# Seven products instead of eight for half a batch, one wait of a block sum cut to what it reads, and a new order table

## The chip, the cores and the metric

The kernel runs on one core of a Trainium2 chip. The metric is the device time of one execution in microseconds (us), the median of several runs. A core has five engines that run side by side, each working through its own instructions in order: TensorE (PE in the profile; its weight loads are PEld), VectorE (DVE), ScalarE (ACT), GpSimd (POOL) and SyncE (SP). POOL and SP here do little but start transfers. The engines meet at semaphores.

## The reference, cut to what matters

Attention of 8 batches, 8 heads, 576 positions and head size 64, with a feature map in place of a softmax, then a feed-forward layer over all 4608 tokens.

```python
theta = pi / 2 * arange(S) / S
phi(x) = concat([relu(x) * cos(theta), relu(x) * sin(theta)])   # 64 -> 128
kv  = einsum('bhsf,bhsd->bhfd', phi(k), v);  z = sum(phi(k), over s)
num = einsum('bhsf,bhfd->bhsd', phi(q), kv); den = einsum('bhsf,bhf->bhs', phi(q), z) + 1e-6
x   = (num / den), heads side by side: 4608 tokens x 512
out = relu(x @ w_in) ** 2 @ w_out          # w_in 512 x 2048, w_out 2048 x 512
```

## The kernel before, in words

*Tiling.* Of each batch's 576 tokens 512 are "main" and 64 a "tail"; the tails of all 8 batches form a ninth batch (`b` = 8) of the feed-forward part. Main tokens are two sets of 256 (`tok` 0 and 1), made of the position groups `j` = 0 to 3. Inputs are float32; products run in bf16 and sum in PSUM.

*Attention of a batch b*, by the names of the steps: `ldk`, `ldq`, `ldv` load; `cos{b}.{j}` and `sin{b}.{j}` make the features, one instruction each on ScalarE or VectorE; `vs{b}.{i}` spreads v beside a column of ones; `kv{b}` is 40 matmuls, `kvz{b}` copies their sums out; `qT` turns the query features (on TensorE for batches 0 and 1, with a copy `qTc`; by a transposing DMA `qTd` on SP's queue later); `num{b}.{j}` is 8 matmuls; `div{b}.{j}` is three VectorE instructions; `xT` and `xTc`, later `xTd`, turn x. There is one PSUM buffer (pool `n`) for `kz` and `num`, so each `num` waits for the division before it.

*First matmul of the feed-forward part.* A plain block `H{b}.{s}.{tok}{half}` (`plan_plain1`) is 8 matmuls of 128x256 for 256 hidden units and 256 tokens, then a relu (`...r`) and for each two blocks a square (`...q`). A slice s takes four such blocks. Alternatively (`plan_gemm1`) a slice is done as a 2 x 2 block product in seven products `G{b}.{s}.P1` to `P7` of 4 matmuls each. These need sums of blocks of x (`xs{b}.1` to `4`, on VectorE) and of w_in (`w1s1` to `4`), and running sums that leave PSUM between products: `seed` and the copies `u2` and `s5`, then `c11` and `c21` (a relu) and `c12` and `c22` (a sum and a relu in one VectorE instruction). The tuple `PLAIN` names the (batch, half of the slices) that are done plainly; batch 0 always is.

*Second matmul.* `Y0.a0` to `a15` and `Y0.b0` to `b15` for batch 0: two matmuls of 128x512 each, for hidden block 0 to 15, for tokens set 0 (a) and 1 (b). Step n needs quarter n // 4 of w_out. Then `Y1` to `Y8` in seven products again, with sums `Y{b}.S1` to `S4` of activations and sums `w2t1` to `w2t4` of w_out (`plan_w2_sums`, L1333).

*PSUM* has a pool `x` of six banks for all else, `hps`, `ha`, `hb`, `hc`, transposes and second sums; a step that takes a bank waits for its last reader.

*What sets the order.* `ORDER` (L23 to L116) is a table of about 1070 step names. The planner `Plan.run` walks it: a word's star means ScalarE, and each engine gets its steps in the table's order. Its own durations and the given landing times of the first loads (for example q of batch 1 at 30.2, and the quarters of w_out at 27.4, 37.0, 41.9 and 45.2) only decide which buffer of a pool a step takes. The engines run their lists on the chip by semaphores.

*Start.* `begin()` does the first part of batch 0 by hand and puts on POOL's queue k tails, q and v of batch 0, four quarters of w_in (512 KB in bf16 each) and the first quarter of w_out. `loads_of_1()` puts there q and k of batch 1 with tails, w_out's second quarter, v of batch 1 and the last two quarters. It is called from the emission loop, not from the table:

```python
for o in order:
    ...
    o.emit(o.engine)
    if o in first:          # cos0.2, sin0.2, cos0.3, sin0.3
        first.remove(o)
        if not first:
            loads_of_1()
```

Loads of batch 2 are table words (`ldv2.0`, `ldk2`, ...) on POOL's queue too; from batch 3 on they stand on SP's. POOL's DMAs use eight semaphores in turn, so each waits for the one eight places before it to land.

Of the kernel before, what the change touches and what calls it, by code (L numbers as in the profile page):

```python
# [35 lines left out]
xT1.2 xTc1.2 Y0.a12 ldk2 Y0.a13 Y0.a14 Y0.b12 Y0.b13 w2t3 xT1.0 xTc1.0 Y0.a15 xTc1.1* vs2.0*
num1.3 Y0.b14 div1.3 Y0.c01* Y0.b15 Y0.c10* Y0.c11 Y0.c00* cos2.1 ldqt3 sin2.0 H1.3.00.0 sin2.1
cos2.3 xT1.3 xTc1.3* sin2.3 ldqt2 H1.3.00r* H1.2.00.0 H1.2.00r* ldkt2 H1.2.10.0 ldv2.1 vs2.1
H1.1.10.0 H1.1.11.0 H1.1.00.0 cos2.0* sin2.2* H1.0.11.0 H1.1.11r* H1.0.01.0 cos2.2* H1.1.00r*
ldkt3 sin2.tk* H1.2.10r* H1.3.10.0 H1.0.11r H1.3.10r* H1.2.01.0 Y0.st1 H1.1.10r* H1.0.01r  # L40
cos2.tk kv2 w2t2 w2t4 H1.1.11q H1.3.10q* kvz2* H1.2.01r* H1.0.10.0 H1.0.10r Y0.st0 qTd2.0
# [6 lines left out]
kv3 xTc1.4* H2.0.01.0 H2.1.00r xs2.4 Y1.c110* H2.0.00r* H2.1.00q* Y1.s5* G2.2.P1 H2.0.01r* kvz3
Y1.c22 G2.2.seed qTd3.0 num3.0 div3.0 cos3.tq* sin3.tq H2.1.11.0 H2.1.11r* H2.1.11q H2.0.10.0
H2.0.10r* num3.1 qTd3.1 H2.1.01.0 div3.1 Y1.P3 num3.2 H2.1.10q* ldq4 w1s3 G2.2.P2 Y1.c12  # L50
H2.1.01r* H2.1.01q* G2.2.P6 G2.2.c11r* div3.2 ldv4.0 G2.2.u2 G2.2.P5 G2.3.P1 ldk4 num3.3 div3.3
vs4.0* qTd3.2 ldkt4 G2.3.P5 G2.2.P7 G2.3.seed G2.2.s5* G2.2.c22r xTd3.0 G2.3.P2 G2.3.P6 G2.3.s5*
G2.3.P3 ldv4.1 G2.2.P4 G2.2.P3 G2.3.u2 G2.3.c11r* G2.3.P7 cos4.3 num3.4 G2.3.c11q Y2.P1 cos4.0
sin4.1* G2.2.c21r* G2.3.c22r G2.2.c12r sin4.0 cos4.1* cos4.2* G2.3.P4 G2.3.c21r xTd3.1 ldv5.2
G2.3.c12r sin4.2 xs3.1 sin4.3* ldkt5 Y1.st0 Y1.P4 Y2.seed G2.3.c21q* G2.3.c22q* G2.3.c12q Y2.S1
G3.0.P1 G3.0.seed qTd4.0 Y1.c21* qTd4.1 Y2.P2 G3.0.P2 xs3.2 G3.0.c11r* G3.0.P5 xs3.3 G3.1.P1
G3.0.P6 G3.0.s5* cos4.tk* G3.1.P5 Y2.S2 G3.0.u2* div3.4 G3.0.P3 Y2.P6 sin4.tk* vs4.1 kv4
G3.0.c12r Y2.u2 G3.1.seed G3.1.P2 Y2.S3 ldk5 G3.1.P6 vs5.2* kvz4* Y2.c11* Y2.S4 G3.0.P7 num4.0
G3.0.c22r ldv5.0 G3.1.c11r* G3.1.c11q* Y2.P5 xs3.4 G3.0.P4 G3.2.P1 div4.0 ldq5 G3.1.u2* G3.1.s5*
ldqt5 vs5.0* Y1.st1 G3.0.c21r num4.2 div4.2 G3.1.P3 Y2.s5 G3.1.P7 G3.1.c22r G3.1.c12r Y2.P7  # L60
num4.1 div4.1 ldqt6 G3.2.seed ldv5.1 G3.1.P4 G3.1.c21r* G3.2.P6 G3.2.u2* ldqt4 G3.2.P2 G3.2.c11r
sin5.0 Y2.c22 Y2.P3 Y2.c12 cos5.3* num4.3 G3.2.P5 G3.3.P1 G3.3.P5 cos5.1* xTd4.0 div4.3 xTd4.1
G3.2.s5* G3.3.seed G3.2.P7 G3.2.c22r G3.2.P3 G3.2.c12r sin5.1 G3.3.s5* G3.3.P6 Y2.st0 G3.3.u2*
cos5.0 qTd5.0 G3.3.P2 G3.3.c11r* G3.3.c11q G3.2.P4 G3.3.P3 G3.3.P7 Y2.P4 G3.3.c22r vs5.1* sin5.3
cos5.2 G3.1.c12q* G3.3.P4 Y3.P1 G3.1.c21q* G3.3.c21r G3.3.c12r G3.3.c12q sin5.2* kv5 xs4.1
G3.2.c21r* G3.3.c21q xs4.2 G4.0.P1 G4.0.P5 qTd5.1 ldv6.0 G3.3.c22q* Y3.seed Y3.P2 cos5.tq*
sin5.tq* kvz5* G3.1.c22q Y3.S1 Y3.S2 xs4.3 num5.0 div5.0 xs4.4 G4.0.seed G4.0.P2 G4.0.s5* ldv6.2
G4.0.P3 Y2.c21* G4.1.P1 G4.0.c11r* G4.0.P6 G4.0.u2* G4.0.c12r ldk6 Y3.S4 Y3.P6 ldq6 G4.1.seed
G4.1.P2 G4.1.c11r* G4.0.P7 G4.1.P6 G4.1.u2* G4.0.c22r vs6.2* num5.2 Y3.S3 G4.1.P5 G4.2.P1
Y3.c11* G4.0.P4 G4.1.P7 G4.1.s5* div5.2 Y3.P5 G4.1.c22r G4.1.c22q num5.3 div5.3 G4.1.P4 G4.1.P3  # L70
G4.0.c21r* G4.1.c12r Y3.u2* G4.2.seed G4.2.P6 G4.2.P2 vs6.0* G4.1.c21r* num5.1 G4.2.u2*
G4.2.c11r div5.1 G4.2.P5 G4.3.P1 G4.2.s5 ldkt6 sin6.3 sin6.0* qTd5.2 G4.3.seed Y2.st1 sin6.1
cos6.2* cos6.1* cos6.3* Y3.P7 Y3.s5 Y3.c22 G4.3.P6 G4.2.P3 cos6.0 G4.3.u2* xTd5.1 G4.2.P7
G4.2.c22r ldkt7 ldv6.1 G4.3.P2 xTd5.0 Y3.P3 G4.3.c11r* G4.3.c11q G4.3.P5 qTd6.0 G4.1.c21q*
G4.3.s5* G4.2.P4 G4.3.P7 Y3.c12 Y3.st0 G4.2.c21r* G4.3.P3 Y3.P4 sin6.2 qTd6.1 G4.3.c22r ldk7
G4.3.P4 G4.3.c12r vs6.1 G5.0.P1 xs5.3 ldv7.0 cos6.tk* sin6.tk* kv6 xs5.1 Y3.c21* G4.2.c12r xs5.2
G5.0.P5 G5.0.seed G5.1.P1 G5.0.P2 G4.1.c12q G4.3.c22q* ldq7 G4.1.c11q kvz6* G4.3.c21r num6.0
div6.0 G5.0.P6 G5.1.seed G5.1.P2 G5.1.P6 G4.3.c12q* Y4.S1 Y4.P1 G5.0.s5* Y4.S3 G5.0.u2* xTd3.2
num6.1 div6.1 G5.0.P3 G5.0.c12r G5.0.c11r* G4.3.c21q* Y4.S2 Y3.st1 G5.0.P7 Y4.seed Y4.P2
G5.1.c11r* ldqt7 xs5.4 G5.1.P5 G5.2.P1 G5.1.u2* G5.0.c22r G5.1.P7 num6.2 div6.2 G5.1.s5*  # L80
G5.1.c22r G5.1.P3 Y4.c11* G5.1.c12r vs7.0 G5.1.c22q* G5.0.P4 G5.0.c21r Y4.P6 Y4.u2* G5.2.P5
G5.2.s5* num6.3 G5.1.P4 ldv7.1 G5.2.seed G5.1.c11q Y4.P5 cos7.2* G5.2.P6 G5.1.c21r* G5.2.u2*
div6.3 Y4.S4 G5.2.P2 G5.2.c11r* cos7.3* cos7.1 G5.2.P3 sin7.2 G5.2.c12r Y4.s5* sin7.0 Y4.P7
# [1538 lines left out]
```

## Time and profile before

| | |
|---|---|
| median of 3 runs | 272.52 us (272.49 to 272.57) |
| the profiled execution | 271.95 us |
| its span, first to last instruction | 269.9 us |
| TensorE busy | 263.1 us (97%), 2787 matmuls |
| VectorE busy | 228.1 us (85%) |
| ScalarE busy | 186.7 us (69%) |
| POOL busy (it starts transfers) | 26.9 us (10%) |
| DMA | 51.23 MB, mean 190 GB/s |
| granted TensorE clock | 1.00 throughout |

Busy time counts from an instruction's start to its end, and matmuls overlap, so a busy TensorE says little by itself; whether it waits is seen from the starts of its matmuls. "Released by" says which engine or transfer ended a wait. The chain of waits is followed back from the last instruction, at each step to what let it go. In a timeline row the first two numbers are start and length in us, and the brackets give idle time before and what ended it. A DMA row of issues ends with the median time from issue to landing.

### The profile page before, as it was taken

Reading aid. Unit: us, or ns where it says so; the run is one execution under the profiler, and the core shown is the slowest. Engines: PE = TensorE matmul, PEld = TensorE weight load, DVE = VectorE, ACT = ScalarE, POOL = GpSimd, SP = SyncE. Lnnn points to the kernel's source line nnn. Section 1 sums busy time; section 2 is a strip of 40 time slices with the busy share of each in tenths; the row PEclk is TensorE's granted clock in tenths of the full one; section 3 lists DMA queues with packets and bytes.
Section 4 is the critical chain, followed back from the end, with each engine's and each line's share of the span. In section 5 each row is a group of like instructions: output and inputs, shape, how many; then the busy total and the mean of one; then the engine's idle time right before and its main releaser. Section 6 shows DMA issues by size and latency. Waiting matters only on the chain.

```text
span 269.9 us, 6751 instructions
## 1 busy us (share of the span) xinstructions
PE 263.1 (97%) x2787; PEld 225.0 (83%) x2792; DVE 228.1 (85%) x412; ACT 186.7 (69%) x289; POOL 26.9 (10%) x44
## 2 busy tenths in 40 slices
PE   8899999999999999999999999999999999999994
PEld 3568856699899889989998998899888888888883
DVE  3877987889998999999999999899978858797941
ACT  4762695698888997689699868587658636755510
POOL 8934443200000000000000000000000000000000
PEclk9999999999999999999999999999999999999999
DMA  6999999999899999999899998652540111010115
GB/s 221 220 206 253 328 198 250 298 295 298 221 247 314 221 261 298 300 183 231 284 275 209 232 359 208 152 155 100 61 125 15 38 63 78 8 72 2 78 50 186
DMA packets 82367, 51.23 MB, mean 190 GB/s; under 512 B 53217, under 2 KB 78817, under 8 KB 82337
## 3 DMA queue, kind: packets, MB, share of 16 engines
q1 hardware_dynamic: 71008, 38.28, 55.5%
q0 software_dynamic: 10736, 12.00, 21.2%
q10 hardware_dynamic: 592, 0.52, 0.6%
q8 instruction: 22, 0.36, 0.6%
q14 instruction: 9, 0.07, 0.1%
HBM read 36.70 MB, written 9.44 MB: 171 GB/s over the span
## 4 chain that ended last, share of the span: by engine, by line
PE 83%; DMA 12%; POOL 3%; issue 0%; DVE 0%; POOLq 0%
PE ya L461 18%; PE yb L461 16%; PE hb L461 13%; PE ha L461 8%; PE hc L461 8%; PE hps L461 8%; DMA w1sb<-in_moe_w_in_dram 5%; DMA kq<-in_k_dram 4%; PE num L461 3%; DMA w2sb<-in_moe_w_out_dram 3%; PE kz L461 3%; PE yc L461 3%; PE yh L461 3%; POOL kq L509 1%; POOL w1sb L411 1%; POOL v L1378 1%
## 5 line engine op out<-in xcount | busy, mean ns | idle before, releaser
L461 PEld LDWEIGHTS <-w1sb 128*128 128x128 bf16 x736 | 70.4, 98 | 8.6
L461 PEld LDWEIGHTS <-gs 128*128 128x128 bf16 x512 | 49.9, 98 | 5.8
L461 PEld LDWEIGHTS <-gT 128*128 128x128 bf16 x448 | 43.1, 98 | 9.8 <-issue 0.2
L442 ACT ACTIVATE gT<-gT 128x1024 bf16<-128x1024 bf16 x38 | 39.5, 1059 | 3.4 <-DVE gT L455 1.8
L461 PE MATMUL hps<-xT,w1sb 128*128 128x256 bf16 x320 | 37.4, 273 | 0.0
L448 ACT ACTIVATE fe<-kq,cols 128x1024 bf16<-128x1024 f32 (+1 forms) x39 | 35.1, 950 | 2.8 <-DMA kq<-in_k_dram 1.7
L461 PEld LDWEIGHTS <-w1s 128*128 128x128 bf16 x312 | 29.7, 98 | 3.3
L461 PE MATMUL ya<-w2sb,gT 128*128 128x256 bf16 x256 | 30.7, 273 | 0.0
L461 PE MATMUL hb<-xs,w1sb 128*128 128x256 bf16 x208 | 30.6, 273 | 0.0
L450 DVE TENSOR_SCALAR fe<-kq,cols 128x1024 bf16<-128x1024 f32 (+1 forms) x41 | 26.9, 690 | 4.0 <-DMA kq<-in_k_dram 4.0
L461 PE MATMUL ha<-xT,w1sb 128*128 128x256 bf16 x176 | 26.2, 273 | 0.0
L444 DVE TENSOR_TENSOR gT<-gT 128x1024 bf16<-128x1024 bf16 x34 | 23.2, 686 | 1.2 <-ACT gT L436 0.8
L436 ACT ACTIVATE gT<-ha 128x512 bf16<-128x512 f32 x21 | 12.6, 601 | 15.9 <-PE ha L461 15.9
L633 DVE TENSOR_TENSOR xp<-num,den 128x512 bf16<-128x512 f32 (+1 forms) x33 | 22.2, 675 | 1.1
L436 ACT ACTIVATE gT<-hps 128x512 bf16<-128x512 f32 x26 | 15.4, 602 | 8.1 <-PE hps L461 8.0
L455 DVE CUSTOM_DVE_ANT_0 gT<-hb,s 128x512 bf16<-128x512 f32 x26 | 17.8, 686 | 3.7 <-PE hb L461 3.3
L458 DVE TENSOR_TENSOR gs<-gT 128x2048 bf16<-128x2048 bf16 x16 | 19.4, 1219 | 0.4
L455 DVE CUSTOM_DVE_ANT_0 gT<-hc,u 128x512 bf16<-128x512 f32 x26 | 17.7, 683 | 0.8 <-PE hc L461 0.8
L432 ACT COPY hb<-ha 128x512 f32<-128x512 f32 x26 | 15.2, 585 | 4.3 <-DVE gT L438 1.8
L461 PE MATMUL hb<-xs,w1s 128*128 128x256 bf16 x104 | 15.6, 273 | 0.0
L436 ACT ACTIVATE gT<-hb 128x512 bf16<-128x512 f32 x18 | 10.8, 599 | 7.0 <-PE hb L461 4.5
L461 PE MATMUL hc<-xs,w1s 128*128 128x256 bf16 x104 | 15.6, 273 | 0.0
(120 smaller groups left out, 415.7 us busy)
## 6 DMA issues: line engine op xcount, KB each, us to landing
out_dram<-y SPq DMA_DIRECT2D x16, 512.0 KB, 3.7
vs<-in_v_dram SPq DMA_DIRECT2D x10, 512.0 KB, 4.8
kq<-in_k_dram SPq DMA_DIRECT2D x5, 1024.0 KB, 7.1
...
```

The costliest lines, as they stand in the source:

```text
L411: nc.gpsimd.dma_start(out=w1sb[:, :, f0:f1], in_=moe_w_in[:, f0:f1].rearrange("(kb p) f -> p kb f", p=P),)
L432: (nc.scalar.copy if e == "ACT" else nc.vector.tensor_copy)(out=out, in_=in_)
L436: nc.scalar.activation(out=out, in_=in_, func=ACTF.Relu)
L442: nc.scalar.activation(out=out, in_=in_, func=ACTF.Square)
L444: nc.vector.tensor_tensor(out=out, in0=in_, in1=in_, op=ALU.mult)
L448: nc.scalar.activation(out=out, in_=in_, func=ACTF.Relu, scale=col)
L450: nc.vector.tensor_scalar(out=out, in0=in_, scalar1=0.0, scalar2=col, op0=ALU.max, op1=ALU.mult)
L455: nc.vector._custom_dve(dve_ops.TENSOR_ADD_SAT, out=out, in0=in0, in1=in1, s0=BIG, s1=0.0)
L458: nc.vector.tensor_tensor(out=out, in0=in0, in1=in1, op=op)
L461: nc.tensor.matmul(out=out, lhsT=lhsT, rhs=rhs, start=start, stop=stop, skip_group_check=True)
L509: eng.dma_start(out=kq[b][:, "kq".index(nm)][:, hs, js], in_=main_of(nm, b)[:, hs, js])
L633: nc.vector.tensor_tensor(out=x, in0=n4[:, :, :, 0:D].rearrange("p b (k l) d -> p b k l d", l=2), in1=r.rearrange("p b (k l) -> p b k l", l=2)
```

## The change

1. `PLAIN` loses (2, 0): slices 0 and 1 of batch 2 are done by `plan_gemm1` instead of `plan_plain1`. The steps `H2.0.*` and `H2.1.*` go, and `G2.0.*` and `G2.1.*` come. The sum `w1s3`, which overwrites a block of w_in that plain blocks read, no longer waits for them but for those of batches 0 and 1 alone.
2. `w2t1`, the first block sum of w_out, waits for quarters 0 and 1 of w_out, which hold its two blocks; before it waited for all four.
3. The whole table `ORDER` is another one. Its beginning and the parts that the prediction speaks of:

```diff
-PLAIN = ((1, 0), (1, 1), (2, 0))
+PLAIN = ((1, 0), (1, 1))
...
-                w2_in + [made[a] for a in after] + (plain if n == 3 else []),
+                w2_in[: 2 if n == 1 else 4]
+                + [made[a] for a in after]
+                + (plain if n == 3 else []),
...
-sin0.2* xT0.k0 sin0.3 xT0.k2 cos0.2* qT0.2 cos0.3* qT0.3 xT0.k3 xTc0.k0 qTc0.2 num0.2 div0.2
-H0.1.00.0 xTc0.k2* H0.1.00.1 ldv2.0 H0.0.00.0 H0.0.00.1 xTc0.k3 xT0.2 qTc0.3* num0.3 H0.1.00.2
-H0.0.00.2 H0.2.00.0 div0.3 xT0.3 H0.3.00.0 xTc0.3 xTc0.2* H0.1.10.0 H0.1.10r H0.0.00r H0.1.00r*
+cos0.2* sin0.2* ldv2.0 xT0.k0 xTc0.k0* xT0.k2 sin0.3 xT0.k3 cos0.3 qT0.2 qT0.3 xTc0.k3*
+H0.0.00.0 qTc0.2 num0.2 xTc0.k2 H0.0.00.1 H0.0.00.2 H0.1.00.0 H0.1.00.1 H0.1.00.2 div0.2 xT0.2
+qTc0.3* xTc0.2* num0.3 H0.2.00.0 H0.2.00r* div0.3 xT0.3 xTc0.3 H0.3.00.0 H0.3.00r* H0.0.10.0
...
-Y0.a11 div1.1 num1.2 div1.2 Y0.b9 Y0.b10 Y0.b11 ldq2 w2t1 xT1.1 num1.0 H0.3.01q* div1.0 vs2.2
+sin1.1k cos1.tk* vs1.1 kv1 qTc1.2* H0.1.11q Y0.b8 Y0.b9 kvz1* num1.1 div1.1 Y0.a8 Y0.a9 ldv2.2
...
-num2.0 div2.0 vs3.0* Y1.P21 Y1.c111* Y1.S2 Y1.S3 cos3.1* ldv4.2 Y1.P5 cos3.0 sin3.0* sin3.1
-sin3.2 xTd2.1 num1.4 cos3.3* Y1.P6 H2.1.10.0 Y1.u2 H2.0.11.0 sin3.3* cos3.2 H2.1.10r* Y1.P7
+num2.0 Y1.S1 div2.0 Y1.P21 Y1.S2 ldq3 sin3.0* sin3.3* w1s3 Y1.P5 num1.4 div1.4 Y1.P6 Y1.u2*
+ldv3.1 vs3.1 xTd2.1 sin3.2 xT1.4 xTd2.0 xs2.1 sin3.1 xs2.2 Y1.c111 xs2.4 cos3.1* G2.0.P1 Y1.P7
+G2.0.seed G2.0.P6 xs2.3 G2.0.P5 ldqt3 cos3.0* G2.0.u2* G2.0.s5* xTc1.4* cos3.2 G2.0.P2
+G2.0.c11r* cos3.3 G2.0.P7 G2.0.c22r ldqt2 ldv4.2 G2.0.P3 G2.0.c12r G2.1.P1 G2.1.seed G2.0.P4
+G2.0.c21r* Y1.S4 G2.1.P5 G2.1.s5* G2.1.P2 G2.1.c11r* G2.1.P6 G2.1.u2* G2.1.P3 kv3 ldv4.0 kvz3*
+qTd3.0 G2.1.c11q G2.1.c12r cos3.tq* sin3.tq G2.1.P7 G2.1.c22r num3.0 div3.0 G2.2.P1 qTd3.1
```

More of the change, by code (lines that the diff above doesn't have):

```diff
@@ L36 @@
[L36 to L41, printed above, removed]
@@ L48 @@
[L48 to L53, printed above, removed]
@@ L54 @@
[L54 to L83, printed above, removed]
@@ new lines @@
+H0.1.00q H0.1.10r H0.1.10q H0.3.11.0 H0.3.11r f0.t1* w1s1 H0.3.10q* H0.1.01.0 H0.1.01r f0.t0*
+qT0.4 H0.1.11.0 H0.1.11r* H0.0.11.0 H0.0.11r* cos1.2q* H0.3.01.0 qTc0.4* sin1.1q sin1.2q*
+H0.3.01r Y0.a0 Y0.a1 Y0.a2 sin1.0q Y0.a3 cos1.3q cos1.0q* H0.2.11.0 qT1.0 qTc1.0 sin1.tq*
+H0.2.01.0 H0.2.11r cos1.tq* qT1.4 cos1.1q* qT1.1 qTc1.4 H0.2.01r* H0.3.01q cos1.3k* qT1.2
+cos1.2k* Y0.b0 Y0.b1 qTc1.1 sin1.tk* Y0.b2 sin1.2k* Y0.b3 H0.3.00q cos1.1k* H0.1.01q Y0.a4 Y0.a5
+Y0.b4 Y0.b5 Y0.a6 w1s2 sin1.0k Y0.a7 sin1.3k vs1.0* Y0.b6 vs1.2 Y0.b7 cos1.0k* sin1.3q* qT1.3
@@ new lines @@
+H1.1.11r* H1.0.10r* H1.1.10r* H1.1.01.0 H1.1.01r* H1.0.11r sin2.tk* H1.3.10.0 H1.1.11q Y0.st0
+H1.3.10r* H1.3.00q* H1.0.01.0 H1.0.01r* kv2 kvz2* H1.1.00.0 H1.2.10r* w2t4 H1.1.00r* H1.0.00.0
+H1.0.00r* H1.1.00q* H1.1.01q qTd2.0 num2.1 qTd2.1 H1.2.01.0 H1.1.10q H1.2.11.0 vs3.2* H1.2.01r*
+H1.3.10q div2.1 H1.2.11r* num2.2 H1.3.11.0 H1.3.11r* Y1.S3 ldv3.0 div2.2 vs3.0 H1.3.01.0
+H1.3.01r* H1.3.01q* Y1.P10 Y1.seed H1.3.11q num2.3 div2.3 Y1.P11 ldk3 Y1.seed1 Y1.P20 Y1.c110*
+num2.0 Y1.S1 div2.0 Y1.P21 Y1.S2 ldq3 sin3.0* sin3.3* w1s3 Y1.P5 num1.4 div1.4 Y1.P6 Y1.u2*
@@ new lines @@
+Y1.c12 num3.2 div3.2 G2.2.P2 G2.1.c21r* G2.1.c21q ldq4 G2.2.P6 G2.2.c11r* G2.3.P1 G2.3.P5 num3.3
+div3.3 G2.2.u2* G2.2.P7 G2.3.seed G2.3.P6 G2.3.P2 G2.2.c22r vs4.2 G2.3.s5* G2.3.P3 G2.3.u2*
+G2.3.P7 G2.2.P4 G2.3.c11r* G2.2.c21r* G2.2.P3 ldk4 cos4.1* G2.3.c11q ldkt4 sin4.1* Y2.P1
+G2.3.c22r G2.3.P4 qTd3.2 G2.3.c21r* Y2.seed xTd3.0 num3.4 cos4.0 G2.3.c21q* G2.3.c22q* sin4.0
+ldkt5 G2.3.c12r Y1.P4 xTd3.1 G2.2.c12r cos4.3 G2.3.c12q ldv4.1 sin4.3* G3.0.P1 G3.0.seed xs3.1
+G3.0.P5 Y1.c21* Y2.P2 cos4.2 ldqt4 G3.0.s5* G3.0.P2 G3.0.c11r* xs3.2 G3.0.P6 Y1.st0 G3.0.u2*
@@ L116 @@
+G8.3.P7 Y7.S3 G8.3.c11q* G8.3.c22r G8.1.c12q Y7.P3 Y7.c12 G8.3.c22q* G8.2.c21r* G8.3.P4 G8.3.P3
+G8.3.c12r G8.3.c12q* Y7.st0 Y8.P10 Y8.seed Y8.P11 G8.1.c22q Y8.seed1 G8.1.c21q* G8.3.c21r*
+G8.3.c21q* Y8.S1 Y8.S2 Y8.S4 Y7.P7 Y7.c22 Y8.P5 Y8.s5* Y8.P6 Y8.u2* Y8.P3 Y8.S3 Y8.P7 Y8.c22
+Y7.P4 Y7.c21* Y8.c12 Y8.st001 Y8.st011 Y8.st111 Y8.st101 Y7.st1 Y8.P4 Y8.c21* Y8.st110 Y8.st100
+Y8.P20 Y8.c110 Y8.st0010 Y8.st0000 Y8.P21 Y8.c111 Y8.st0100 Y8.st0110
 """
-PLAIN = ((1, 0), (1, 1), (2, 0))
+PLAIN = ((1, 0), (1, 1))
```

105 lines of the change are left out of this document (61 added, 44 removed).

## The prediction

> **What bounds the kernel now.** I read the page's busy shares first, then the waits of TensorE alone, then the chain of waits over the first 50 us, then the DMA queues in short stretches, and last the timeline of VectorE where the change puts its new work.
>
> ```profile
> span 269.9 us, 6751 instructions
> PE 263.1 (97%) x2787; PEld 225.0 (83%) x2792; DVE 228.1 (85%) x412; ACT 186.7 (69%) x289; POOL 26.9 (10%) x44
> ```
>
> ```profile
> PE wm L461 <- DVE zeros L362: 1.2, 1, 1.2
> PE tq L1428 <- DVE fe L450: 0.7, 1, 0.7
> PE num L461 <- ACT kvz L432: 0.2, 1, 0.2
> ```
>
> These three waits are all that TensorE shows, and all lie before 13 us. From 50 us on matmul follows matmul: I found no space between starts that is wider than the tile before it explains by more than 0.1 us. So every microsecond taken from TensorE's work is won and every new wait is lost, one for one. One place is an exception, in the chain of waits:
>
> ```profile
> 9.42 12.43 DMA w1sb<-in_moe_w_in_dram
> 21.85 0.28 issue
> 22.13 11.36 DMA kq<-in_k_dram
> 33.49 0.28 issue
> 33.77 9.04 DMA w2sb<-in_moe_w_out_dram
> 42.81 0.04 issue
> 42.85 0.38 PE yh L461
> ```
>
> The third quarter of w_out (operand `w2sb`) lands at 42.81 and TensorE starts its first product with it (`Y0.a8`) 0.04 later. Before it stood eight transposes from 42.14, 0.45 long, so TensorE was free at 42.59: 0.26 of waiting, too short for the list above. The queue that brings it is full. Queue q0, POOL's, in the stretches 14 to 18 us and 41 to 42 us (packets, MB, time as a share of 16 engines):
>
> ```profile
> q0 software_dynamic: 813, 0.81, 122.5%
> ```
>
> ```profile
> q0 software_dynamic: 199, 0.20, 120.7%
> ```
>
> Every stretch that I asked for between 14 and 43 us shows 105% or more for this queue. What is put into it early therefore delays all that stands behind.
>
> **The change, part by part.**
>
> *Fewer products.* Plain blocks of batch 2, slices 0 and 1 (`H2.0`, `H2.1`), were 8 steps of 8 matmuls; in seven products they are 14 steps of 4. That is 64 against 56. The chain prices 16 such matmuls (128x256) at 1.75, so 8 cost 0.87: the gain is 0.87 us on TensorE. Evictions grow: 8 (a relu each) become 14, the six new ones being copies (0.58 on ScalarE), and four relus become sums with a relu that only VectorE does (0.68). Squares stay 4. Over the kernel the built order gives ScalarE 13 instructions more and VectorE 7 fewer; VectorE's are cheap features and copies that moved to ScalarE. This costs nothing by itself where VectorE has room; where it has none, see below.
>
> *The first block sum of w_out.* `w2t1` now waits for two quarters instead of four. In the trace it started at 46.74 straight behind a division that ended at 46.83 and after the last quarter was there, and in the new table it stands later (behind `div1.3`). Nothing waited, so I price it at 0; a gain is excluded because VectorE runs in order, a loss because a wait only goes.
>
> *The table, start.* Up to the transpose `xT0.3` both orders give TensorE the same steps, but two quarter steps stood between `num0.3` and it and now stand ahead of it. By rows: division 1.13 plus 0.20 release, against 0.87 of cover (`H0.2.00.0`); `xT0.3` comes at about 20.8 instead of 20.61. This 0.2 is inside the 0.26 of idle time at 42.59, so 0.
>
> *The table, POOL's queue.* The loads of batch 1 are emitted when the four query features `cos0.2`, `sin0.2`, `cos0.3`, `sin0.3` are out. In the old table that is word seven, ahead of `ldv2.0`. In the new one `ldv2.0` (half of v of batch 2) is word three, and the built order shows it on POOL straight behind the first quarter of w_out, ahead of q1, k1, quarter two, v1 and quarters three and four of w_out. Its price: two equal loads that follow each other,
>
> ```profile
> 27.58 0.76 POOL L526 DMA_DIRECT2D vs<-in_v_dram x1 [0.83 <-DMA w2sb<-in_moe_w_out_dram]
> 30.56 0.74 POOL L526 DMA_DIRECT2D vs<-in_v_dram x1 [2.23 <-DMA kq<-in_q_dram]
> ```
>
> whose rows of issues say 9.9 and 8.2 to landing, so 37.5 and 38.8: 1.3 apart. The one before (a quarter of w_out, 25.97 and 10.2, so 36.2) leaves 1.35. I take 1.35. Low end 0, if the queue had holes, against which the shares above speak. High end 2.6: each POOL load also waits for the one eight places ahead, and with one more in the ring k1 waits for the fourth quarter of w_in (issued 10.15, 14.3 to landing) instead of the third (21.85); if its 11.36 were fixed and not time in the queue, everything would shift by those 2.6. First user of quarter three is now `Y0.b8`, with exactly as much TensorE work ahead of it as `Y0.a8` had. q1, too, is 1.35 later: `cos1.2q` at 31.65 on ScalarE, then `qTc0.4`, whose PSUM slot `H0.2.11.0` needs, and `cos1.0q`, which `qT1.0` needs: TensorE waits some 0.65 there, but that is earlier and so inside the 1.35. VectorE and POOL behind gain slack. Cost: 1.35.
>
> The Trainium skill, "DMA: Bandwidth & Descriptors", section "Anatomy of one DMA", puts a load of this path at 2.0 us fixed plus its bytes by 436 GB/s, an estimate of 3.2 for the 512 KB that are read here. Taken as time in the queue it would give 275.9 in place of my figure; the landings 1.3 apart say that the fixed part overlaps. The same page, section "SWDGE vs HWDGE vs iDMA", says only one such queue is allocated; the trace agrees, as its loads landed in order of issue.
>
> *The table, 70 to 88 us.* VectorE is full here already:
>
> ```profile
> 70.00:80.00 10.00, 10.00 (x112) 8.83 (x111) 9.86 (x16) 8.76 (x12) 0.00 (x0) 1.00 0.90 202
> ```
>
> (The stretch, its length, then busy time of PE, PEld, DVE, ACT and POOL, the clock, the DMA share and GB/s.) Starts follow each other like this:
>
> ```profile
> 71.05 0.16 DVE L627 TENSOR_SCALAR den<-num 128x8 f32<-128x8 f32 x1
> ...
> 72.09 1.22 DVE L458 TENSOR_TENSOR gs<-gs,gT 128x2048 bf16<-128x2048 bf16 x1
> 73.22 1.22 DVE L458 TENSOR_TENSOR gs<-gT 128x2048 bf16<-128x2048 bf16 x1
> 74.36 2.07 DVE L450 TENSOR_SCALAR fe<-kq,cols 128x1024 bf16<-128x1024 f32 x3
> ```
>
> A division is 1.04, a block sum 1.13, a feature 0.66, an eviction of 512 0.60, an x sum 0.33. Four waits of TensorE follow, each counted from the one before:
>
> (a) `G2.0.P6` needs the second x sum. VectorE from the end of `num2.3`: release 0.20, `div2.3` 1.04, `Y1.S1` 1.13, `div2.0` 1.04, `Y1.S2` 1.13, `w1s3` 1.13 (moved here from 87.18), `div1.4` 1.04, `vs3.1` 0.60, `sin3.2` 0.66, `xs2.1` 0.33, `sin3.1` 0.66, `xs2.2` 0.42, 0.05 to TensorE: 9.43. TensorE meanwhile: 3 x 0.87, 3 x 1.75, the two `num` 0.25 and 0.53, a transpose 0.22, `G2.0.P1` 0.44: 9.30. Late by 0.13.
> (b) `G2.0.P4` needs `G2.0.c22r`, behind `Y1.c111` 0.36, two x sums, two features and itself 0.68: 2.98 against 2.67. Late by 0.31.
> (c) `G2.1.P5` takes the bank that `G2.0.c12r` frees: 0.60 against 0.44. Late by 0.16.
> (d) `num3.0` needs `kvz3`: release 0.20, copy 0.59, 0.05, with one product (0.44) between. Late by 0.40.
>
> Sum 1.00. Low end 0.40: only (d) needs no queue of VectorE. High end 2.2: `G2.0.P1` now needs the transposes by DMA of both halves of x2 at about 77; the last is issued at about 73.9, and such rows run from 2.75 to 4.9 to landing, 1.2 late at worst. I take 1.00, since the 4.9 stood behind a v load that now goes earlier. `H2` steps that hid these chains (0.87 each with one eviction) are gone, so this cover is not there.
>
> *Later than 100 us.* Handovers with little cover (a product that waits for an eviction one product earlier) are as many and as short in the new order as in the old, which shows no wait. I price this at 0, with 0 to 0.5.
>
> Sum: -0.87 + 1.35 + 1.00 = +1.48. Against the profiled execution's own 271.95 (span 269.9 and 2.05 around it) that is 273.4; it stood 0.57 under the median of the runs, 272.52, so I predict 274.0.
>
> **The rivals.**
>
> *The shift is larger.* The ring of eight lets the delay grow to 2.6, or the transposes come 1.2 late: 275.2 to 275.3, both 276.5. For it: the chain runs over just those waits. Against: the queue holds several loads at each of them.
>
> *The early load is hidden.* Then -0.87 + 1.00 leaves +0.13: 272.65, no change. Against: shares over 105%.
>
> *The saving arrives: faster.* Place: VectorE's queue at `num2.3`. If features on ScalarE leave it with 0.6 us of slack there, (a) to (c) vanish, and with w_out on time only (d) stays: -0.47, 272.05; -0.87, 271.65, if `kvz3` is covered as well. It decides where lateness at `Y0.b8` and waits at 77 to 88 us sum to under 0.33. Against: 9.86 of 10 us busy.
>
> *The change does not do what it says*: true of `w2t1`, and worth nothing either way.
>
> **How the numbers follow.** Both delays as sized, within 273.3 to 274.9: 0.62. Larger shift: 0.19. Hidden load, about 272.4 to 273.0: 0.12. Faster: 0.07. Changes under 0.2% (0.54 us) are no change that a measurement of this kernel can tell. Hidden load splits, 0.07 to within and 0.05 to slower; so faster 0.07, same 0.07, slower 0.86. The range 272.6 to 275.7 leaves out the faster case, a part of the hidden load and the two mishaps together.
>
> **What would show it.** Right: `Y0.b8` starts at about 44.2, straight upon a landing of w_out; q1's first feature at 31.6; spaces between matmuls at 80 to 88 us that sum to about 1, with `num` waiting for `kvz`. Wrong: w_out's third quarter landing at 43 or earlier, TensorE without spaces at 77 to 88 us, or new ones beyond 100 us, which I did not price.

## The result and the profile after

The changed kernel takes 275.26 us (median of 4 runs, 274.75 to 275.78) against 272.50 for the kernel before in the same comparison: a ratio of 1.0099, 95% interval 1.0076 to 1.0123, or 2.76 us slower. The profiled execution took 275.01, 3.06 more than that of before. The page of the changed kernel:

```profile
span 272.9 us, 6743 instructions
PE 263.5 (97%) x2779; PEld 224.0 (82%) x2784; DVE 223.8 (82%) x405; ACT 191.1 (70%) x302; POOL 26.9 (10%) x44
```

The eight matmuls are gone (2787 to 2779), and yet TensorE is busy 0.4 longer: busy time hides both the saving and the waits. These are shown by the view of TensorE's waits, which before ended at 13 us (it counts only what exceeds a usual handover, so it reads lower than the spaces between starts that the text quotes):

```profile
PE kz L462 <- DVE vext L433: 0.6, 2, 0.4
PE num L462 <- ACT kvz L433: 0.5, 2, 0.2
PE tq L1431 <- ACT fe L449: 0.5, 1, 0.5
PE ha L462 <- DMA xT<-xp: 0.4, 1, 0.4
PE tx L657 <- DVE xp L634: 0.3, 1, 0.3
PE tq L652 <- ACT fe L449: 0.2, 1, 0.2
```

The rows `kz` and `tq L1431` and one of the two `num` lie before 13 us, where the two kernels do the same work. `tx` is the transpose `xT0.3` at 21.39, with a space of 0.51 ahead of it; `tq L652` is `qT1.0` at 34.68, 0.37; `ha` is `G2.0.P1` at 77.68, 0.55; the other `num` is `num3.0` at 87.07, 0.41. The chain of waits, which before ran over the third quarter of w_out, now runs over q of batch 1, then over a transpose of x2 by DMA, then over `kvz3`:

```profile
18.03 14.14 DMA kq<-in_q_dram
32.17 0.02 issue
32.19 0.54 ACT fe L449
...
73.27 4.37 DMA xT<-xp
77.64 0.04 issue
77.68 0.60 PE ha L462 x4
...
86.42 0.60 ACT kvz L433
87.03 0.04 issue
87.07 0.40 PE num L462 x8
```

The timeline of POOL's issues in the changed kernel (start, length, what is issued, and in brackets the time before it and what ended that) shows the early load between the first quarter of w_out and q1:

```profile
12.71 0.76 POOL L419 DMA_DIRECT2D w2sb<-in_moe_w_out_dram  x1 [0.30 <-DMA v<-in_v_dram]
15.16 0.75 POOL L527 DMA_DIRECT2D vs<-in_v_dram  x1 [1.70 <-DMA w1sb<-in_moe_w_in_dram]
18.03 0.90 POOL L510 DMA_DIRECT2D kq<-in_q_dram  x1 [2.12 <-DVE xT L433]
```

Last, a place that the prediction did not look at, the end. The timelines of VectorE and of SP's stores in the changed kernel (ScalarE's queue starts about as many stores, at nearly the same times):

```profile
262.79 0.69 DVE L459 TENSOR_TENSOR y<-yb,ys 128x512 f32<-128x512 f32 x1 [2.56 <-issue]
263.39 0.68 DVE L459 TENSOR_TENSOR y<-yc,yu 128x512 f32<-128x512 f32 x1
267.97 0.42 DVE L433 COPY y<-ya 128x256 f32<-128x256 f32 x1 [0.45 <-PE ya L462]
```

```profile
264.10 1.34 SPq L1107 DMA_DIRECT2D out_dram<-y  x2
265.53 0.62 SPq L1098 DMA_DIRECT2D out_dram<-y  x1
266.83 2.67 SPq L1107 DMA_DIRECT2D out_dram<-y  x3
```

and the same two in the kernel before:

```profile
259.16 0.69 DVE L458 TENSOR_TENSOR y<-yc,yu 128x512 f32<-128x512 f32 x1 [1.27 <-issue]
260.85 0.69 DVE L458 TENSOR_TENSOR y<-yb,ys 128x512 f32<-128x512 f32 x1 [1.00 <-PE yb L461]
266.09 0.42 DVE L432 COPY y<-ya 128x256 f32<-128x256 f32 x1 [0.45 <-PE ya L461]
```

```profile
259.88 2.31 SPq L1106 DMA_DIRECT2D out_dram<-y  x2
263.20 0.34 SPq L1097 DMA_DIRECT2D out_dram<-y  x1
264.95 2.07 SPq L1106 DMA_DIRECT2D out_dram<-y  x3
```

The new table puts `Y8.c12` (`y<-yc,yu`) behind `Y8.c22` (`y<-yb,ys`), `Y7.P4` and `Y7.c21`. Early stores that went out from 259.88 on now go out from 264.10 on and meet the last ones: the last three issues on SP take 2.67 in place of 2.07, the last store is issued 0.56 after its copy has ended (268.39 to 268.95; before 0.03, from 266.51 to 266.54) and lands 2.81 after its issue in place of 2.02. From the start of the last matmul to the end of the span it is 5.21 us, before 4.13.

So the 3.0 us of the span are: TensorE's last matmul 1.88 later, the end 1.08 longer. The 1.88 divide at the first product with w_out's third quarter, ahead of which both orders give TensorE the same work. It is now `Y0.b8`; the row of TensorE's timeline that starts with it:

```profile
43.98 1.02 PE L462 MATMUL yh<-w2sb,gT 128*128 128x512 bf16 x3
```

`Y0.a8` started at 42.85, so this is 1.13 later. From there to the last matmul 0.76 are lost, the saved 0.87 against 1.63 of new spaces, 1.49 of them between 70 and 90 us.

### The profile page after: what moved, and what is told of

Its sections match the earlier page's. It is cut to its first block, busy times and chain, and to the rows that moved or that the text cites. A ratio compares the mean times of both kernels' runs of the same rounds, so it can differ in the third digit from the quotient of the medians.

```text
span 272.9 us, 6743 instructions
## 1 busy us (share of the span) xinstructions
PE 263.5 (97%) x2779; PEld 224.0 (82%) x2784; DVE 223.8 (82%) x405; ACT 191.1 (70%) x302; POOL 26.9 (10%) x44
## 4 chain that ended last, share of the span: by engine, by line
PE 83%; DMA 10%; ACT 2%; POOL 2%; DVE 1%; issue 0%; POOLq 0%
PE ya L462 17%; PE yb L462 15%; PE hb L462 13%; PE hc L462 9%; PE ha L462 9%; DMA kq<-in_q_dram 8%; PE hps L462 5%; PE yh L462 4%; PE kz L462 3%; PE num L462 3%; PE yc L462 2%; DMA xT<-xp 2%; ACT fe L449 1%; PE tq L652 1%; POOL v L1381 1%; POOL kqt L513 1%
## 5 line engine op out<-in xcount | busy, mean ns | idle before, releaser
L462 PEld LDWEIGHTS <-w1sb 128*128 128x128 bf16 x704 | 67.2, 98 | 9.0 <-issue 0.9
L449 ACT ACTIVATE fe<-kq,cols 128x1024 bf16<-128x1024 f32 (+1 forms) x42 | 38.6, 959 | 2.9 <-DMA kq<-in_q_dram 1.6
L462 PEld LDWEIGHTS <-w1s 128*128 128x128 bf16 x336 | 32.3, 98 | 3.9 <-issue 0.2
L443 ACT ACTIVATE gT<-gT 128x1024 bf16<-128x1024 bf16 x31 | 32.3, 1059 | 1.6 <-DVE gT L456 1.1
L462 PE MATMUL hps<-xT,w1sb 128*128 128x256 bf16 x256 | 29.8, 273 | 0.2
L462 PE MATMUL ha<-xT,w1sb 128*128 128x256 bf16 x192 | 28.6, 272 | 0.4 <-DMA xT<-xp 0.4
L445 DVE TENSOR_TENSOR gT<-gT 128x1024 bf16<-128x1024 bf16 x41 | 27.6, 684 | 1.5 <-ACT gT L437 0.9
L451 DVE TENSOR_SCALAR fe<-kq,cols 128x1024 bf16<-128x1024 f32 (+1 forms) x38 | 23.6, 657 | 3.9 <-DMA kq<-in_k_dram 3.2
L433 ACT COPY u<-hb 128x512 f32<-128x512 f32 x21 | 12.4, 590 | 11.4 <-PE hb L462 11.4
L437 ACT ACTIVATE gT<-ha 128x512 bf16<-128x512 f32 x24 | 14.5, 605 | 5.2 <-PE ha L462 5.0
L433 ACT COPY s<-hc 128x512 f32<-128x512 f32 x24 | 14.1, 588 | 4.3 <-PE hc L462 4.3
L437 ACT ACTIVATE gT<-hps 128x512 bf16<-128x512 f32 x23 | 13.0, 598 | 5.9 <-PE hps L462 5.5
```

Of the source, the lines that this page charges most:

```text
L433: (nc.scalar.copy if e == "ACT" else nc.vector.tensor_copy)(out=out, in_=in_)
L437: nc.scalar.activation(out=out, in_=in_, func=ACTF.Relu)
L443: nc.scalar.activation(out=out, in_=in_, func=ACTF.Square)
L445: nc.vector.tensor_tensor(out=out, in0=in_, in1=in_, op=ALU.mult)
L449: nc.scalar.activation(out=out, in_=in_, func=ACTF.Relu, scale=col)
L451: nc.vector.tensor_scalar(out=out, in0=in_, scalar1=0.0, scalar2=col, op0=ALU.max, op1=ALU.mult)
```

## The experiments

Ratios are to the kernel before on the same chip, with a 95% interval. Waits and landings are those of one profiled execution each; executions of one kernel differ among themselves by 1 to 3 us, and when transfers land differs with them. Where a version is compared with the changed kernel, both intervals count, so such a difference is uncertain by some 0.9 us.

**The early load in the kernel before, alone.**

```diff
-sin0.2* xT0.k0 sin0.3 ...
+sin0.2* xT0.k0 ldv2.0 sin0.3 ...
...
-H0.1.00.0 xTc0.k2* H0.1.00.1 ldv2.0 H0.0.00.0
+H0.1.00.0 xTc0.k2* H0.1.00.1 H0.0.00.0
```

> The kernel before with one word moved: ldv2.0 becomes the table's third word, so POOL issues it ahead of the loads of batch 1. Theory: w_out's third quarter lands 1.3 us later, and as TensorE was at most 0.3 us short of it, the kernel is 1.0 to 1.4 us slower, 273.5 to 273.9. Rival (hidden load): within 0.3 us of 272.5.

Measured: 273.74, ratio 1.0054 (1.0036 to 1.0072), about 1.5 slower. The price is there, with nothing else of the change. The chain of waits of this run now goes over q of batch 1:

```profile
17.67 14.38 DMA kq<-in_q_dram
32.05 0.03 issue
32.08 0.72 ACT fe L449
32.80 0.49 ACT gT L437
33.29 0.04 issue
33.33 1.91 PE hps L462 x16
```

ScalarE runs in order: the relu (`gT`, L437) that frees TensorE's bank stands behind the first feature of q1, which waits for q1. TensorE waits 0.87 ahead of `H0.3.01.0`, and only some 0.15 at w_out's third quarter. Still it is this quarter that sets the price: issued at 35.47, it landed after 8.60, at 44.07 (before: 42.81), and `Y0.a8` started at 44.11, 0.04 later, just as before. By an estimate from these numbers, without the wait for q1 TensorE would have come there at about 43.1 and waited 1.0 instead of 0.15. The two waits stand in series, and the second is too short here for the chain to show it.

Landings counted from that of w_out's first quarter, which is ahead of them all, show the shift free of when an execution got going. In the seven profiled executions with the early load q1 landed 4.28 to 4.77 after it, in the seven without 2.91 to 3.47; the third quarter 15.9 to 17.3 after it against 14.5 to 15.5. In the mean each is 1.4 later. The Trainium skill's estimate quoted in the prediction (3.2 from "DMA: Bandwidth & Descriptors", "Anatomy of one DMA") is too large as the delay that a load brings to those behind it in this queue: that was 1.4 in the mean.

**The load put back in the changed kernel.**

```diff
-cos0.2* sin0.2* ldv2.0 xT0.k0 xTc0.k0* xT0.k2 sin0.3 xT0.k3 cos0.3 qT0.2
+cos0.2* sin0.2* xT0.k0 xTc0.k0* xT0.k2 sin0.3 xT0.k3 cos0.3 ldv2.0 qT0.2
```

> The changed kernel with one word moved: the first v load of batch 2 (ldv2.0) stands behind cos0.3 again, so POOL issues it behind the loads of batch 1 and w_out, as before the change. Theory of the prediction (w_out's third quarter held TensorE back by 1.35): 1.3 us faster than the changed kernel, about 273.9. Rival read from the trace of the changed kernel (the third quarter landed at 43.9 and TensorE came there at 44.2, so only the two waits on q1 at 33 to 35 us, 0.4 to 0.6 together, hang on the load): 0.4 to 0.6 faster, about 274.7. If the load were hidden: no change, 275.3.

Measured: 274.92, ratio 1.0092 (1.0070 to 1.0114): some 0.2 faster than the changed kernel, not 1.3 (the intervals admit 0.7 slower to 1.1 faster, so the rival's 0.4 to 0.6 stays possible). The rival rests on a start of `Y0.b8` at 44.2, but its first matmul is at 43.98, 0.13 after the landing, so by the trace the waits on q1 alone were worth some 0.1. From the view of TensorE's waits in it:

```profile
PE ha L463 <- DMA xT<-xp: 0.8, 1, 0.8
...
PE yh L463 <- DMA w2sb<-in_moe_w_out_dram: 0.3, 1, 0.3
```

In this execution there are 0.44 at `Y0.b8`, now waiting for the quarter of w_out as the kernel before did, and at `G2.0.P1` the space grew from 0.55 to 0.92. It was the longest of the six (276.01), so it doesn't show by itself where the gain of the others went; that it is lost at `G2.0.P1`, behind the early load in series, is borne out by the version with start, load and end put right.

**The end put back in the changed kernel.**

```diff
-Y8.P7 Y8.c22 Y7.P4 Y7.c21* Y8.c12 Y8.st001 Y8.st011 Y8.st111 Y8.st101 Y7.st1
+Y8.P7 Y8.c12 Y8.st001 Y8.st011 Y8.c22 Y7.P4 Y7.c21* Y8.st111 Y8.st101 Y7.st1
```

> The changed kernel with Y8.c12 and its two stores moved ahead of Y8.c22, as in the kernel before. Theory: the four early stores go out at about 261 and 264 us instead of 264.1 to 265.3, the last stores find a free queue, and the time from the last matmul's start to the end falls from 5.2 to about 4.1: 1.1 us faster, about 274.2. Rival: the long end is a chance of that one profiled execution, and the time stays within 0.3 us of 275.3.

Measured: 274.23, ratio 1.0067 (1.0047 to 1.0087), 0.9 faster than the changed kernel. From the last matmul to the end of the span it is 4.12, as in the kernel before. All other waits of the changed kernel are still there (0.51 at `xT0.3`, 0.78 at `G2.0.P1`, 0.41 at `num3.0`), and a new one came: 0.52 at 101 us, where `G3.0.P5` waits for an x sum of batch 3.

**The new end in the kernel before**, first with only half of it, then whole.

```diff
-Y8.P7 Y8.c12 Y8.st011 Y8.c22 Y8.st001 Y8.st111 Y8.st101 Y7.P4 Y7.c21* Y7.st1
+Y8.P7 Y8.c22 Y8.st111 Y8.st101 Y7.P4 Y7.c21* Y8.c12 Y8.st001 Y8.st011 Y7.st1
```

> The kernel before, with only the end of the table in the changed kernel's order: Y8.c12 and its stores behind Y8.c22, Y7.P4 and Y7.c21. Theory (the late copy crowds the last stores): the four early stores go out some 4 us later and meet the last ones on SP, the last store is issued late and lands later; last matmul to end of span grows from 4.1 to about 5.1 us, 1.0 slower than the kernel before. Rival (the 1.08 at the end of the changed kernel is chance of one profile, or comes from its later arrival there): no change, within 0.3 us.

Measured: 272.66 against 272.04, ratio 1.0017 (0.9999 to 1.0035); last matmul to end 4.37. The edit left the two stores `Y8.st111` and `Y8.st101` early. With these moved as well:

```diff
-Y8.P7 Y8.c12 Y8.st011 Y8.c22 Y8.st001 Y8.st111 Y8.st101 Y7.P4 Y7.c21* Y7.st1
+Y8.P7 Y8.c22 Y7.P4 Y7.c21* Y8.c12 Y8.st001 Y8.st011 Y8.st111 Y8.st101 Y7.st1
```

> The kernel before, with Y8.c12 and now all four early stores behind Y8.c22, Y7.P4 and Y7.c21, the very order of the changed kernel's end. Theory (four early stores, not two, have to go out late to crowd the last ones): they are issued from 2.8 us before the last matmul on, the last store lands late, last matmul to end of span some 5.2 in place of 4.1: 1.0 slower than the kernel before. Rival (the order of the copies is worth what moving two stores gave, 0.24 in the span and 0.5 in the time, and the rest of the changed kernel's 1.08 has another cause): 4.4 and 0.5 slower at most.

Measured: 272.96, ratio 1.0023 (1.0006 to 1.0040), 0.6 slower than before; last matmul to end 4.97. The mechanism holds: the more stores are left to the last 3 us, the later the last one lands. The interval admits 0.2 to 1.1, and 0.84 of the profile's 1.08 is reproduced.

**Start, load and end put right together in the changed kernel**, and one feature (`cos3.3`) that stood ahead of a sum TensorE needs.

```diff
-cos0.2* sin0.2* ldv2.0 xT0.k0 ...
+cos0.2* sin0.2* xT0.k0 ... cos0.3 ldv2.0 ...
-H0.0.00.0 qTc0.2 num0.2 ... H0.0.00.2 ... H0.1.00.2 div0.2 ... num0.3 H0.2.00.0
+qTc0.2 num0.2 H0.0.00.0 ... div0.2 ... num0.3 H0.0.00.2 H0.1.00.2 H0.2.00.0
-G2.0.c11r* cos3.3 G2.0.P7 G2.0.c22r ... G2.0.c12r
+G2.0.c11r* G2.0.P7 G2.0.c22r ... G2.0.c12r cos3.3
...
```

> The changed kernel with four moves in the table: ldv2.0 back, the tail's sums and stores ahead, at the start H0.0.00.0 behind num0.2 and H0.0.00.2, H0.1.00.2 behind num0.3 (as in the kernel before), and cos3.3 behind G2.0.c12r. Theory: 1.1 from the tail, 0.5 to 1.3 from the load, 0.3 from the start, 0.2 from the feature: 2.1 to 2.9 faster than the changed kernel, 272.4 to 273.2, near the kernel before; what is left against a gain of 0.87 are the waits for the transposes of x2 (0.55) and for kvz3 (0.4). Rival (the moves only shift waits): 274 or more.

Measured: 274.31, ratio 1.0067 (1.0046 to 1.0088): no better than the end alone. The wait 0.51 at `xT0.3` fell to 0.08, TensorE came to `G2.0.P1` at 76.3 instead of 77.1, and waited there for 1.34; 0.52 are again at `G3.0.P5`. Its chain of waits:

```profile
72.39 5.17 DMA xT<-xp
77.56 0.04 issue
77.60 0.60 PE ha L463 x4
```

This and the load put back say the same: what comes from ahead of 77 us is lost at `G2.0.P1`. Its start lay between 77.3 and 78.2 in all executions that have it in this place. The twelve times of this version lie between 272.7 and 275.1; the profile is of one at 274.37, and what was different in the fastest isn't known.

**Cover for that wait by order alone.** `G2.0.P1` behind `Y1.P7`, 1.75 of other work.

```diff
-cos3.1* G2.0.P1 Y1.P7
+cos3.1* Y1.P7 G2.0.P1
```

> The changed kernel, with only G2.0.P1 behind Y1.P7 instead of ahead of it, so that 1.75 us of other work cover the transposes of x2 by DMA. Theory (that wait costs one for one): the 0.55 at G2.0.P1 goes, G2.0.P6 behind it would come at 79.3 where its x sum is ready at 79.2, so nothing takes its place: 0.5 faster than the changed kernel, some 274.7. Rival (VectorE is full, so the wait moves on to G2.0.P6 and G2.0.P4, which need its x sums and its sum with a relu): no change, waits at these two that sum to 0.5 more.

Measured: 277.04, ratio 1.0165 (1.0136 to 1.0193), slower. The wait for x2 went, and two took its place, in the view of TensorE's waits from 70 to 90 us:

```profile
PE hb L463 <- ACT hb L434: 0.7, 1, 0.7
PE yb L463 <- ACT yu L434: 0.5, 1, 0.5
```

`Y1.P7` needs the copy `Y1.u2` of the step just ahead (a space of 0.67), and `G2.0.P6` needs `G2.0.seed`, the copy of what `G2.0.P1` has just made (0.82). With 0.23 at the next copy (`G2.0.u2`) and 0.48 at `G3.0.P5` that is close to the 1.8 by which it is slower than the changed kernel. In the table's order each of the two products covered the other's copy. Neither theory had this: the wait moved, but to ScalarE's copies, not to VectorE's sums.

**One product more between `kv3` and `num3.0`.**

```diff
-G2.1.P6 G2.1.u2* G2.1.P3 kv3 ldv4.0 kvz3* qTd3.0
+G2.1.P6 kv3 kvz3* G2.1.u2* G2.1.P3 ldv4.0 qTd3.0
```

> The changed kernel, with only kv3 and kvz3 one product earlier (ahead of G2.1.P3, 0.44 us), so that two products stand between kv3 and num3.0. The planner's buffers then differ for 101 later steps. Theory: the 0.41 at num3.0 goes and the division behind it starts 0.4 earlier too: 0.4 faster than the changed kernel, some 274.9. Rival (the chain of num and div of batch 3 is bound at its other end): the wait turns up at num3.1 or behind, no change.

Measured: 276.53, ratio 1.0148 (1.0122 to 1.0174), slower. The edit put `kvz3` ahead of `G2.1.u2` on ScalarE, and `G2.1.P7`, which needs `u2`, waited 0.89; `num3.1` waited 0.60 for VectorE. With `kvz3` left behind it:

```diff
-G2.1.P6 G2.1.u2* G2.1.P3 kv3 ldv4.0 kvz3* qTd3.0
+G2.1.P6 G2.1.u2* kv3 G2.1.P3 ldv4.0 kvz3* qTd3.0
```

> The changed kernel with kv3 alone one product earlier; its copy kvz3 stays behind G2.1.u2 on ScalarE, unlike in the run before. Theory A (num3.0 waits for the copy and for nothing else): the 0.41 goes and is won, 0.4 faster than the changed kernel. Theory B (VectorE is the bound there: G2.1.c12r, sin3.tq and G2.1.c22r stand ahead of div3.0 and one product later than before): div3.0 starts where it did, num3.1 waits some 0.45 in place of 0.08, no change from the changed kernel within 0.3.

Measured: 276.12, ratio 1.0133 (1.0107 to 1.0158), no gain. `num3.0` no longer waits, `num3.1` and `G2.1.P4` do (0.61 and 0.49). TensorE's waits from 80 to 95 us:

```profile
PE num L463 <- DVE xp L635: 0.4, 1, 0.4
PE hb L463 <- DVE gT L457: 0.3, 1, 0.3
```

Both are for VectorE, whose timeline has no gap from 86.14 on (and one of 0.81 just before, ended by a product of TensorE that now stands behind `kv3`):

```profile
86.14 0.69 DVE L457 CUSTOM_DVE_ANT_0 gT<-hc,u 128x512 bf16<-128x512 f32 x1 [0.81 <-PE hc L463]
86.75 0.48 DVE L452 TENSOR_SCALAR fet<-kqt,cols 128x512 bf16<-128x512 f32 x1
87.14 0.68 DVE L457 CUSTOM_DVE_ANT_0 gT<-hb,s 128x512 bf16<-128x512 f32 x1
87.74 0.16 DVE L629 TENSOR_SCALAR den<-num 128x8 f32<-128x8 f32 x1
```

`num3.0` ended at 86.56, and its division (last row) began 1.18 later, behind two sums and a feature; in the changed kernel it began 0.17 after the end of `num3.0` (87.34 to 87.51). Of the two, theory B names the mechanism: covering the copy alone doesn't win the 0.41, since VectorE comes to the division just as late. Its forecast of no change is not met as well; the median is some 0.9 slower than the changed kernel (interval 0 to 1.9), and the profiled execution (275.05) was the fastest of the five. And as VectorE was idle ahead of this stretch, it is the order of its steps that is late there; a division ahead of the two sums was not tried.

**All of the above together**, with two edits at 94 to 101 us (`ldkt5` behind `xTd3.1`, `Y2.P2` ahead of `G3.0.P5`).

> The changed kernel with all of it together: ldv2.0 behind cos0.3, the old order of the last copies, two quarter steps of batch 0 behind num0.3 and one behind num0.2, cos3.3 behind G2.0.c12r, G2.0.P1 behind Y1.P7, kv3 one product earlier, ldkt5 behind xTd3.1 and Y2.P2 ahead of G3.0.P5. Theory (seven products save 0.87 and all the rest was the table's): w_out's third quarter binds at 43 as in the kernel before, then -0.87 and the small waits left (0.22 at Y1.P20, 0.25 at G2.0.P4 and G2.1.P5, 0.1 elsewhere): 0.3 faster than the kernel before, and 2.5 to 3 faster than the changed kernel. Rival (VectorE's fuller queue takes the saving wherever the steps stand): 0.5 slower than the kernel before or worse, with waits between 70 and 90 us that sum to over 1.4.

Measured: 275.92, ratio 1.0127 (1.0097 to 1.0158). It holds both misplaced moves, `G2.0.P1` behind `Y1.P7` and `kvz3` ahead of `u2`, and shows their waits again (0.67, 0.82, 0.90, 0.61 and smaller ones). The time is as the rival had it, but these waits are for copies on ScalarE and for the order on VectorE, so it does not tell the two theories apart.

**Is it the load ahead in SP's queue that holds up the transposes?** The last load of v of batch 3 goes behind them.

```diff
-ldv3.1 vs3.1 xTd2.1 sin3.2 xT1.4 xTd2.0 xs2.1
+xTd2.1 sin3.2 xT1.4 xTd2.0 ldv3.1 xs2.1
...
-cos3.3 G2.0.P7
+cos3.3 vs3.1 G2.0.P7
```

> The changed kernel with the last load of v of batch 3 (ldv3.1) behind the transposes xTd2.1 and xTd2.0 on SP's queue, and its spreading vs3.1 behind cos3.3 on VectorE. No order on TensorE changes. Theory (the transposes of x2 land late because that load of 0.5 MB fills the queue ahead of them): xTd2.0 lands some 3.3 us after its issue in place of 4.4, at 76.6, the 0.55 at G2.0.P1 goes, and of it 0.1 comes back at G2.0.P4: 0.4 to 0.5 faster than the changed kernel. Rival (transposes take that long whatever is ahead of them): it lands at 77.6 as before, no change, or 0.15 slower for the later vs3.1.

Measured: 280.37, ratio 1.0287 (1.0261 to 1.0314). On the question itself the rival is right: `xTd2.0` took 4.15 from issue to landing with that load behind it, against 4.37. Most of the 5 us come from a queue that the edit did not count, SP's. Its timeline in this run:

```profile
77.49 0.59 SPq L521 DMA_DIRECT2D vst<-in_v_dram  x1
82.58 0.37 SPq L528 DMA_DIRECT2D vs<-in_v_dram  x1
83.05 6.62 SPq L671 DMA_TRANSPOSE qpT<-fe  x2
```

SP runs in order. `ldv4.0` (82.58) waits for the buffer that `vs3.1` frees, and `vs3.1` now runs at 81.86. Behind it stands `qTd3.0`, which was issued at 83.05 instead of 80.38 and landed after 7.34, with that load issued 0.47 ahead of it, instead of 3.81. `num3.0` waited 3.26 for it. The rest of this execution's new waits: 1.42 at `G3.3.P1` (125 us), behind features of q of batch 5, which landed at 122.86; 0.89 at `Y0.b8`, for a landing ahead of the edit; and 0.38 at `G3.0.P5`.

**The transposes taken off the path.** `G2.0.P1` reads one of the two halves of x2, but its wait names both, and the table transposes the half that it reads last. This version starts from the one with start, load and end put right, adds the two edits at 94 to 101 us, and

```diff
-lambda: blk(0, 0), True, xr + [w[0], begun.get(b - 2)] + seeded[-2:], xb)
+lambda: blk(0, 0), True, x_ready[b, 0] + [w[0], begun.get(b - 2)] + seeded[-2:], xb)
...
-num2.1 ... div2.1 ... num2.2 ... div2.2 ... num2.3 div2.3 ... num2.0 Y1.S1 div2.0
+num2.1 ... div2.1 ... num2.0 ... div2.0 ... num2.2 div2.2 ... num2.3 Y1.S1 div2.3
...
-ldq3 sin3.0* ... ldv3.1 vs3.1 xTd2.1 sin3.2 xT1.4 xTd2.0 xs2.1 sin3.1 xs2.2 Y1.c111 xs2.4
+ldq3 xTd2.0 sin3.0* ... ldv3.1 vs3.1 Y1.c111 sin3.2 xT1.4 xTd2.1 xs2.1 xs2.2 sin3.1 xs2.4
-cos3.1* G2.0.P1 Y1.P7 G2.0.seed
+G2.0.P1 Y1.P7 G2.0.seed cos3.1*
```

> The version that put the start, ldv2.0, the end and cos3.3 right (its G2.0.P1 waited 1.34 and its G3.0.P5 0.52), with the transposes of x2 taken off the path: num and div of batch 2 run in the order 1, 0, 2, 3, so that the half of x2 that G2.0.P1 reads (xTd2.0) is transposed first, and P1 waits for that half alone; xs2.2 stands straight behind xs2.1, Y1.c111 ahead of sin3.2 and cos3.1 behind G2.0.seed; ldkt5 stands behind xTd3.1 and Y2.P2 ahead of G3.0.P5. Theory (what was won earlier was lost at these two waits for transposes): xTd2.0 lands by 73.5, G2.0.P1 does not wait, Y1.P7 0.2 (for Y1.u2) and G2.0.P6 0.3 (for xs2.2), nothing at G3.0.P5: 1.2 to 1.4 faster than that version, 0.4 to 0.7 slower than the kernel before. Rival (VectorE is full there and hands TensorE its work at the same time whatever order stands ahead): G2.0.P6 or G2.0.P4 waits for all of it, no change from that version, 1.8 to 2.0 slower than the kernel before.

Measured: 273.08 against 272.57, ratio 1.0016 (0.9999 to 1.0034): 1.2 to 1.4 faster than the version it starts from, as expected (the intervals admit 0.6 to 2.2), and level with the kernel before within the interval. The view of TensorE's waits between 60 and 100 us is down to one line:

```profile
PE num L463 <- ACT kvz L434: 0.2, 1, 0.2
```

By starts there is 0.23 at `Y1.P7`, 0.11 at `G2.0.P7`, 0.41 at `num3.0` and nothing at `G2.0.P1`, `G2.0.P6` and `G3.0.P5`, where the version it starts from had waited 1.34 and 0.52. Which of its edits is worth how much was not tried. Its profiled execution was one of the longer ones (274.37), with a wait of 1.08 at `G3.3.P1`, at 120 us: q of batch 5 landed at 117.98, features made of it waited on ScalarE and VectorE, and an eviction that frees a bank stood behind them. Whether the other runs had that wait the one profile cannot say.

No version here beats the kernel before. That `w2t1` now waits for two quarters only was not tried by itself, and `G2.0` and `G2.1` were not tried in the old table.

## Why the prediction was right, and where it was not

Forecast 274.0, range 272.6 to 275.7, slower; measured 275.26. The sign is right, and so are two of the causes; the size is 1.3 short. The time lies outside the band of the prediction's main case (273.3 to 274.9) and on the figure of its rival of a larger shift (275.2 to 275.3), but not for that rival's reasons. That the range holds it is in part luck: what the prediction left out happens to be as large as the mishaps for which the range was widened.

By the two profiles its three places compare so: up to the first product with quarter three 1.35 foretold, 1.13 measured; from there to the last matmul -0.87 + 1.00 = 0.13 foretold, 0.76 measured; the end 0 foretold, 1.08 measured. That the first is close is in part chance too: in the changed kernel's profiled execution w_out's first quarter, which is ahead of the early load, already landed 0.6 later (27.89 against 27.29). In the time, moved into the kernel before by themselves, the early load costs 1.47 (1.0 to 2.0) and the end 0.63 (0.2 to 1.1). These do not simply add up with the rest: put back in the changed kernel, the load won only 0.2, the end 0.9.

- *Fewer products, -0.87.* The count of matmuls is as foretold. The saving never shows as time: in the last version, with load, start and end put right, the spaces left between 70 and 90 us sum to 1.3 (0.22 at `Y1.P20`, 0.23, 0.11, 0.08, 0.17, 0.41, 0.08) and outweigh it by 0.4. That version's median is slower than the kernel before by as much, but with an interval from 0 to 0.9 this proves nothing.
- *POOL's queue, 1.35.* Right in size (1.4 between landings, 1.47 in time). In the kernel before with the early load it is right in place as well: `Y0.a8` started straight upon the landing of the quarter, and the wait for q1 lay ahead of it, "inside the 1.35". In the changed kernel it holds but for 0.1: `Y0.b8` started at 43.98 (foretold 44.2), without a wait, 0.13 after the quarter had landed (43.86), since 0.51 at `xT0.3` and 0.63 at the two steps that hang on q1 (33.44 and 34.68) together just exceeded the room ahead of the landing. q1's first feature started at 32.19 on ScalarE, not at 31.65. That TensorE stands at this quarter at all varies from execution to execution: in the two profiles of the kernel before with a new end, whose start is unchanged, the quarter landed 0.31 and 0.59 before TensorE came to it.
- *Start, 0.2 and so 0.* It was 0.51 at `xT0.3`. That it cost little by itself is borne out: taking it away, together with the early load, won nothing that could be told apart. What took it up was not the old 0.26 us at w_out but the later landing there and, behind it, the transposes of x2.
- *70 to 88 us, 1.00.* The mechanism was right, the size was 1.49. (a), 0.13 at `G2.0.P6`, did not come, since `G2.0.P1` waited first. (b) was 0.08, not 0.31. (c) was 0.16, as foretold, and (d) 0.41 against 0.40. Its side remark "only (d) needs no queue of VectorE" fell with the run that moved `kv3`. The transposes of x2, left to the high end because "the 4.9 stood behind a v load that now goes earlier", did bind, for 0.55: `xTd2.0` took 4.15 with the v load behind it, so that reason was wrong. The high end was too low by its own figures as well: 73.9 + 4.9 is 78.8, which is 1.8 behind 77 and not 1.2, and among the transposes of x in the kernel before one took 5.87 (issued at 91.88). 0.22 at `Y1.P20`, behind a seed copy that stands on ScalarE after a square, was not foreseen.
- *Later than 100 us, 0.* Right for TensorE in the profile of the changed kernel: no new space there. But four other versions with the same order at that place show 0.38 to 0.52 at `G3.0.P5`, for the x sum behind a transpose of x of batch 3, so a term of up to 0.5 belongs there, as the prediction's own bound (0 to 0.5) had it.
- *The end.* The sum has no term for it, and this is the term that is missing: 0.6 (put into the kernel before) to 0.9 (taken out of the changed kernel) in time, 1.08 in the profile. The prediction took TensorE's last matmul for the end of the kernel.

The rivals: "the early load is hidden" is refuted by its run in the kernel before; "the saving arrives" by the time of the changed kernel, and no version made from it is faster either. "The shift is larger" was half true. The ring of POOL's semaphores did make the load of k of batch 1 wait, as that rival had it, for the fourth quarter of w_in (landed at 25.05; the load was issued at 25.34, before at 22.13), but then it took 10.08 and not 11.36, so those 11.36 were not fixed, and the landings behind it moved by 1.4 in the mean and not by 2.6. The transposes did come late, by 0.55 and not 1.2.
